# One half of a weight block loaded in a transfer of eight rows by sixteen, and VectorE's work on keys in whole tiles

## The chip, the core and the metric

The kernel runs on one core of one Trainium2 chip. The time is device microseconds (us) of one execution; the times of the kernel before are 663.4, 663.39 and 663.56 us, median 663.4. A core has five engines that each take their own instructions in order: TensorE (PE), VectorE (DVE), ScalarE (ACT), GpSimd (POOL) and SyncE (SP, which here issues almost all transfers). Sixteen DMA engines move data between the chip's large memory and the core's on-chip memory of 128 partitions.

## The reference

Decode of one token for four sequences: attention over a cache, beside a small gated MLP, both added to the input.

```python
x = A_x                                  # (4, 1, 640)
xn = _layernorm(x)
q = (xn @ wq) as 4 x 32 heads x 1 x 128  # wq (640, 4096)
scores = q . k_cache * 128 ** -0.5       # k_cache (4, 32, 4096, 128)
p = softmax(scores)
o = p . v_cache                          # v_cache (4, 32, 4096, 128)
return x + o as (4, 1, 4096) @ wo + _B_ref(xn, w_in, w_sp, b_sp, w_out)   # wo (4096, 640)
```

All inputs are bf16. K and V caches are 134 MB each, so the work is a single pass over 268 MB.

## The kernel before

**Tiles.** The 32 heads form 8 groups of 4 (HT). One tile i is one group and one sequence, hg, b = divmod(i, 4): 32 tiles. A K tile holds 4 heads x 4096 keys x 128 as 128 partitions x 128 keys x 128 (4 MB); 32 partitions (lanes) belong to each head. V tiles are laid out the same way.

**Loads.** K and V tiles share five slots (KV_SLOTS). The order is K0, K1, V0, K2, V1, K3, ... with K one tile further ahead at 24 and 28 (EXTRA_K). pump (L140) issues loads on SP as far as their slots have been used: each load waits for the last reader of the tile five loads earlier. A block of wo (512 rows, 640 KB) is loaded by load_wo (L153) for each group, into two buffers: the 128 partitions hold four rows r each, 5120 bytes in a row of memory (row p * 4 + r of the block). The last block comes in four parts.

**One tile.** Queries stand as rows (qbc), so the scores come from VectorE: product (L455) multiplies the K tile in place by the query row, fold_half (L464) adds the upper 64 of 128 columns to the lower 64, both on one half of the tile (64 keys a lane). sums (L470) lets PE add the remaining 64 columns down to 8, as eight accumulating matmuls against the identity; row_sums (L483) adds the eight on VectorE. lane_max, lay_max, spread_max and head_max (L493 to L518) find the maximum of a head over its lanes (VectorE, ACT, PE, VectorE: m, lay, max_ps, nb). exps (L520) makes p on ACT, and POOL multiplies it by a head mask into pm (L533). blocks (L542) is PE's 32 matmuls of pm with the V tile into pv_acc; after every second tile ACT copies it (pv_sb) and gather (L561) sums it up into pv.

**Groups.** After a group's last tile: group_den (the denominators, rden), group_norm (o_n), group_turn (L612), group_pick (L625) and group_proj (L643). The wo rows of a block lie over partitions as p * 4 + r, so o_n, which has the 128 columns of a head on partitions, must be laid out in the same way. group_turn does it with one matmul for each r against a 0/1 matrix spread[:, r], which takes row m * 4 + r to lane m of each head's 32 lanes; group_pick keeps on each lane the value of its own head (hmask) and sums the four heads away. group_proj multiplies by the wo block into out_ps. The last group needs no turn.

**Order.** The main loop (L677) is written out by hand, and each engine takes its instructions in that order. In iteration i: first half's product of tile i; second half's row sums, maxima and exponentials of tile i - 1, with the first half's fold of i in between; PE's sums for the first half; second product; then blocks, group_den and gather of the tile that is due; row sums of the first half and fold of the second; group_norm; PE's sums of the second half; group_turn; and pump. Which tile is due is in turns (L663): i - 1 up to i = 24, then two, later three behind. Setup runs ahead of the loop: identity, masks, the spread matrices, the layer norm, q, the MLP.

Of the kernel before, what the change touches and what calls it, by code (L numbers as in the profile page):

```python
# [9 lines left out]
FP32 = mybir.dt.float32  # L10
BF16 = mybir.dt.bfloat16
ACT = mybir.ActivationFunctionType
ALU = mybir.AluOpType
AX = mybir.AxisListType

KV_SLOTS = 5
EXTRA_K = (24, 28)
ALIGN = 512


@with_exitstack
def kernel(
# [14 lines left out]
    nc = tc.nc  # L37
    P = nc.NUM_PARTITIONS
    Bsz, Sq, D = A_x.shape
    _, H, S, Dh = A_k_cache.shape  # L40
# [8 lines left out]
    HT = 4  # L49
    HG = H // HT  # L50
    NT = HG * Bsz
    LN = P // HT
    NC = HT * S // P
    HC = NC // 2
    HD2 = Dh // 2
    RW = 8
# [13 lines left out]
    const = ctx.enter_context(tc.tile_pool(name="const", bufs=1))  # L70
    work = ctx.enter_context(tc.tile_pool(name="work", bufs=1))
    small = ctx.enter_context(tc.tile_pool(name="small", bufs=2))
    PSUM = bass.MemoryType.PSUM
    ps_s = ctx.enter_context(tc.tile_pool(name="ps_s", bufs=2, space=PSUM))
    ps_pv = ctx.enter_context(tc.tile_pool(name="ps_pv", bufs=2, space=PSUM))
    ps_m = ctx.enter_context(tc.tile_pool(name="ps_m", bufs=2, space=PSUM))
    ps_out = ctx.enter_context(tc.tile_pool(name="ps_out", bufs=1, space=PSUM))
# [12 lines left out]
    for c0, c1 in ((0, HT), (HT, DC)):  # L90
        t = slot("wq")[:, 0 : (c1 - c0) * HD].rearrange("p (c n) -> p c n", n=HD)
# [13 lines left out]
        out=w_out_sb[:, 0:NFF, :], in_=B_w_out[0 : NFF * P].rearrange("(p k) n -> p k n", k=NFF)  # L105
# [9 lines left out]
    k_tiles, v_tiles = {}, {}  # L115
# [33 lines left out]
    wo_r = A_wo.rearrange("(j p r) n -> j p (r n)", p=P, r=HT)  # L149
    wo_h = A_wo.rearrange("(j h p) n -> j p h n", p=P, h=HT)  # L150
    wo_tiles = {}

    def load_wo(j):  # L153
        wo_tiles[j] = wop.tile([P, HT, D], BF16, name="wo")
        if j == HG - 1:
            for hh in range(HT):
                nc.sync.dma_start(out=wo_tiles[j][:, hh, :], in_=wo_h[j][:, hh, :])
            return
        nc.sync.dma_start(out=wo_tiles[j][:].rearrange("p r n -> p (r n)"), in_=wo_r[j])

    pump()

# [2 lines left out]
    ident = const.tile([P, P], BF16)  # L165
    make_identity(nc, ident[:])
    ident_f = const.tile([P, P], FP32)
# [9 lines left out]
        out=lane_diag[:],  # L177
        in_=ident_f[:].rearrange("p (h l) -> p l h", h=HT),
        axis=AX.X,
        op=ALU.add,  # L180
# [12 lines left out]
    for e in range(2):  # L193
        nc.vector.tensor_reduce(
            out=sel[:, :, :, e],
            in_=ident_f[:].rearrange("p (g e k h) -> p e k h g", g=CG, e=2, k=GC)[:, e],
            axis=AX.X,
            op=ALU.add,
        )

    hmask = const.tile([P, HT], FP32)
    nc.vector.memset(hmask[:], 0.0)
    for hh in range(HT):
        nc.vector.memset(hmask[hh * LN : (hh + 1) * LN, hh : hh + 1], 1.0)
    spread = const.tile([P, HT, HT, LN], BF16)
    nc.vector.tensor_copy(
        out=spread[:],
        in_=ident[:].rearrange("p (m r) -> p r m", r=HT)[:, :, None, :].to_broadcast(
            [P, HT, HT, LN]
        ),  # L210
    )


    q_lanes = const.tile([HT * Bsz, Bsz, P], BF16)
    nc.vector.tensor_copy(
        out=q_lanes[:].rearrange("r b (h l) -> r b h l", h=HT),
        in_=ident[: HT * Bsz, : HT * Bsz]
# [7 lines left out]
    for hh in range(HT):  # L225
        nc.gpsimd.tensor_copy(
            out=place[:, hh, hh * Bsz : (hh + 1) * Bsz], in_=lane_diag[:, 0:Bsz]
# [18 lines left out]
    for i in range(NSTAT):  # L246
# [5 lines left out]
        out=rstd[:], in_=mv[:, 1:2], func=ACT.Sqrt, bias=eps_tile[:Bsz], scale=1.0  # L252
# [4 lines left out]
        out=xn_bf[:],  # L257
# [9 lines left out]
    for c in range(DC):  # L267
        nc.tensor.transpose(
            out=xnT_ps[:, c, :], in_=xn_v[:, c, :], identity=ident[:Bsz, :Bsz]
# [11 lines left out]
    for c in range(DC):  # L281
        t, i = wq_parts[c]
        for hg in range(HG):
            g = hg % CG
# [4 lines left out]
                start=(c == 0),  # L289
# [162 lines left out]
        qbcs[hg] = small.tile([P, Bsz, Dh], BF16, name="qbc")  # L452
        nc.scalar.copy(out=qbcs[hg][:], in_=qb_ps[:])

    def product(i, half):  # L455
        t = k_tiles[i][:, half * HC : (half + 1) * HC, :]
        nc.vector.tensor_tensor(  # L457
            out=t,
            in0=t,
            in1=qbcs[i // Bsz][:, i % Bsz, None, :].to_broadcast([P, HC, Dh]),  # L460
            op=ALU.mult,
        )

    def fold_half(i, half):  # L464
        t = k_tiles[i][:, half * HC : (half + 1) * HC, :]
        nc.vector.tensor_tensor(  # L466
            out=t[:, :, 0:HD2], in0=t[:, :, 0:HD2], in1=t[:, :, HD2:Dh], op=ALU.add
        )

    def sums(i, half):  # L470
        t = k_tiles[i][:, half * HC : (half + 1) * HC, :]
        s = sums_ps[i, half] = ps_s.tile([P, HC, RW], FP32, name="s_ps")
        n = HD2 // RW
        for g in range(n):
            nc.tensor.matmul(  # L475
                out=s[:],
                lhsT=ident[:],
                rhs=t[:, :, g * RW : (g + 1) * RW],
                start=(g == 0),
                stop=(g == n - 1),  # L480
            )

    def row_sums(i, half):  # L483
        if half == 0:
            scores[i] = small.tile([P, NC], FP32, name="s_sb")
        nc.vector.tensor_reduce(  # L486
            out=scores[i][:, half * HC : (half + 1) * HC],
            in_=sums_ps.pop((i, half))[:],
            axis=AX.X,
            op=ALU.add,  # L490
        )

    def lane_max(i):  # L493
# [118 lines left out]
    def group_turn(hg):  # L612

        ps = ps_m.tile([P, HT, HT, Bsz], FP32, tag="m", name="o_ps")
        for r in range(HT):
            nc.tensor.matmul(
                out=ps[:, r, :, :],
                lhsT=spread[:, r, :, :].rearrange("p h m -> p (h m)"),
                rhs=gr[hg][:].rearrange("p h b -> p (h b)"),
                start=True,  # L620
                stop=True,
            )
        gr[hg] = ps

    def group_pick(hg):  # L625
        own = small.tile([P, HT, HT, Bsz], FP32, name="own")
        nc.vector.tensor_tensor(
            out=own[:],
            in0=gr[hg][:],
            in1=hmask[:, None, :, None].to_broadcast([P, HT, HT, Bsz]),  # L630
            op=ALU.mult,
        )
        o_r = small.tile([P, HT, Bsz], BF16, name="o_r")
        with nc.allow_low_precision("one of the four is the value, the others are zeros"):
            nc.vector.tensor_reduce(
                out=o_r[:],
                in_=own[:].rearrange("p r h b -> p r b h"),
                axis=AX.X,
                op=ALU.add,
            )  # L640
        gr[hg] = o_r
# [17 lines left out]
    def at(i, fn, *args):  # L659
        if 0 <= i < NT:  # L660
            fn(i, *args)
# [10 lines left out]
    with tc.manual_schedule(engines={E.PE, E.DVE, E.Activation, E.SP}):  # L672
        stage_q(0)
        gmlp()
        used.update(occupants[:3])
        pump()
        for i in range(NT):  # L677
            j = turns.get(i)
            product(i, 0)
            at(i - 1, row_sums, 1)  # L680
            at(i - 1, lane_max)
            at(i - 1, lay_max)
            at(i - 1, spread_max)
            group(turns.get(i - 1, -1), group_pick)
            if turns.get(i - 1, -1) // Bsz < HG - 2:
                group(turns.get(i - 1, -1), group_proj)
            fold_half(i, 0)
            at(i - 1, head_max)
            at(i - 1, exps)
            sums(i, 0)  # L690
            product(i, 1)
            if i % Bsz == 2 and i // Bsz + 1 < HG:
                stage_q(i // Bsz + 1)
            due = [] if j is None else [j]
            if i == NT - 1:
                due += range(j + 1, NT - 2)
            for n, jj in enumerate(due):
                if n:
                    gather(due[n - 1])
                blocks(jj)  # L700
                group(jj, group_den)
                used.add(("v", jj))
            row_sums(i, 0)
            fold_half(i, 1)
            if due:
                gather(due[-1])
            for jj in due:
                group(jj, group_norm)
            sums(i, 1)
            for jj in due:  # L710
                group(jj, group_turn)
            used.add(("k", i))
            pump()
            if i % Bsz == 2 and i // Bsz < HG - 2:
                load_wo(i // Bsz)
        load_wo(HG - 2)
        load_wo(HG - 1)
        row_sums(NT - 1, 1)
        lane_max(NT - 1)
        lay_max(NT - 1)  # L720
        spread_max(NT - 1)
        head_max(NT - 1)
        exps(NT - 1)
        blocks(NT - 2)
        group_den(HG - 1)
        blocks(NT - 1, 0, V_CUTS[1])
        gather(NT - 1, stop=False)
        for c0, c1 in zip(V_CUTS[1:], V_CUTS[2:]):
            pairs(NT - 1, c0, c1)
        group_norm(HG - 1)  # L730
        group_proj(HG - 2)
        group_proj(HG - 1)

        res = work.tile([P, NOH], BF16, name="res")
        out_v = out.flatten_outer_dims()
        r0, r1 = slice(0, Bsz), slice(OG, OG + Bsz)
        nc.scalar.copy(out=res[r0], in_=out_ps[r0])
        nc.vector.tensor_copy(out=res[r1], in_=out_ps[r1])
        nc.scalar.dma_start(out=out_v[:, 0:NOH], in_=res[r0])
        nc.sync.dma_start(out=out_v[:, NOH:D], in_=res[r1])  # L740
# [30 lines left out]
```

## Time and profile before

| | |
|---|---|
| median of the times | 663.4 us |
| the profiled execution's own time | 663.4 us |
| its span | 661.6 us |
| VectorE busy | 491.5 us, 74% |
| TensorE busy | 348.7 us, 53%; mean granted clock 0.726 |
| GpSimd busy | 151.3 us, 23% |
| ScalarE busy | 49.3 us, 7% |
| moved by DMA | 282.57 MB, mean 427 GB/s |
| q1 (transfers issued by SP) | 11928 packets, 99.2% of 16 engines' span |

The span is from the first to the last instruction of the core; the execution's own time has a little around it. [...] In the groups by line, the number after the bar is busy us and then the mean ns of one instruction; after the second bar comes the idle time of the engine ahead of these instructions, and what ended it. In a timeline each row has start and length in us, engine, line, operation, output and input, count, and in brackets the idle time before and what released it. In the table of stretches the columns are start and end, the length, then for each of PE, PEld, DVE, ACT and POOL its busy us and number of instructions, then the granted clock, the DMA share and GB/s.

### The profile page before, as it was taken

Reading aid. Unit: us, or ns where it says so; the run is one execution under the profiler, and the core shown is the slowest. Engines: PE = TensorE matmul, PEld = TensorE weight load, DVE = VectorE, ACT = ScalarE, POOL = GpSimd, SP = SyncE. Lnnn points to the kernel's source line nnn. Section 1 sums busy time; section 2 is a strip of 40 time slices with the busy share of each in tenths; the row PEclk is TensorE's granted clock in tenths of the full one; section 3 lists DMA queues with packets and bytes.
Section 4 is the critical chain, followed back from the end, with each engine's and each line's share of the span. In section 5 each row is a group of like instructions: output and inputs, shape, how many; then the busy total and the mean of one; then the engine's idle time right before and its main releaser. Section 6 shows DMA issues by size and latency. Waiting matters only on the chain.

```text
span 661.6 us, 5115 instructions
## 1 busy us (share of the span) xinstructions
PE 348.7 (53%) x2109; PEld 144.6 (22%) x2109; DVE 491.5 (74%) x334; ACT 49.3 (7%) x138; POOL 151.3 (23%) x57
## 2 busy tenths in 40 slices
PE   2526653646445455663745654465643756435567
PEld 1402211212121121221212222121211312112124
DVE  2299797867789677788776698776787899777950
ACT  0201100001000010001000000000100000000010
POOL 3002222112222112222112222112222133122230
PEclk9999676776767777766678657777576577688585
DMA  9999999999999999999999999999999999999997
GB/s 368 432 438 429 430 440 427 440 423 434 442 416 447 424 433 442 423 440 424 433 440 423 440 428 431 442 421 442 422 435 442 422 441 428 427 442 428 429 428 289
DMA packets 11971, 282.57 MB, mean 427 GB/s; under 512 B 1344, under 2 KB 1964, under 8 KB 3244
## 3 DMA queue, kind: packets, MB, share of 16 engines
q1 hardware_dynamic: 11928, 282.25, 99.2%
q8 instruction: 16, 0.26, 0.1%
q14 instruction: 7, 0.06, 0.0%
q10 hardware_dynamic: 20, 0.01, 0.0%
HBM read 282.24 MB, written 0.01 MB: 427 GB/s over the span
## 4 chain that ended last, share of the span: by engine, by line
issue 49%; DMA 25%; POOL 15%; DVE 7%; PE 3%; SPq 1%; ACT 0%; POOLq 0%; DVEq 0%; ACTq 0%
DMA k_nat<-in_A_k_cache_dram 20%; POOL pm L533 15%; DMA wo<-in_A_wo_dram 4%; DVE k_nat L457 4%; DVE k_nat L466 2%; PE s_ps L475 2%; PE pv_acc L548 1%; SPq L123 0%; DVE s_sb L486 0%; PE out_ps L647 0%; PE pv L569 0%; POOL own_sum L593 0%; DVE m L495 0%; SPq L92 0%; SPq L104 0%
## 5 line engine op out<-in xcount | busy, mean ns | idle before, releaser
L457 DVE TENSOR_TENSOR k_nat<-k_nat,qbc 128x8192 bf16<-128x8192 bf16 x64 | 282.8, 4419 | 97.8 <-DMA k_nat<-in_A_k_cache_dram 97.8
L533 POOL TENSOR_TENSOR pm<-p,hmask_bf 128x512 bf16<-128x512 bf16 x32 | 142.5, 4452 | 490.9 <-ACT p L524 490.9
L475 PE MATMUL s_ps<-k_nat,ident 128*128 128x512 bf16 x512 | 189.2, 536 | 68.2 <-DVE k_nat L466 68.2
L466 DVE TENSOR_TENSOR k_nat<-k_nat 128x4096 bf16<-128x4096 bf16 x64 | 151.8, 2372 | 0.0
L548 PE MATMUL pv_acc<-v_nat,pm 128*32 128x512 bf16 x1008 | 88.6, 514 | 39.1 <-POOL pm L533 35.5
L508 PE MATMUL max_ps<-lay,head_scale 128*128 128x32 f32 x64 | 18.7, 383 | 171.4 <-ACT lay L501 171.4
L475 PEld LDWEIGHTS <-ident 128*128 128x128 bf16 x512 | 67.9, 135 | 171.1 <-issue 153.8
L508 PEld LDWEIGHTS max_ps<-lay,head_scale 128*128 128x128 f32 x64 | 14.6, 284 | 186.0 <-ACT lay L501 186.0
L548 PEld LDWEIGHTS <-pm 128*32 128x32 bf16 x1008 | 30.2, 120 | 96.2 <-POOL pm L533 52.0
L486 DVE TENSOR_REDUCE s_sb<-s_ps 128x64 f32<-128x512 f32 x64 | 43.3, 677 | 4.2 <-PE s_ps L475 4.2
L501 ACT ACTIVATE lay<-lane_diag,m 128x32 f32<-128x32 f32 x32 | 10.3, 321 | 395.9 <-DVE m L495 395.9
L602 DVE RECIPROCAL rden<-den 128x16 f32<-128x16 f32 x8 | 2.1, 257 | 32.2 <-PE den L600 32.2
L569 PE MATMUL pv<-sel,pv_sb 128*128 128x8 f32 x128 | 19.4, 279 | 9.3 <-ACT pv_sb L558 9.3
L569 PEld LDWEIGHTS pv<-sel,pv_sb 128*128 128x128 f32 x128 | 17.9, 217 | 17.2 <-ACT pv_sb L558 17.2
L524 ACT ACTIVATE p<-s_sb,nb 128x128 bf16<-128x128 f32 x32 | 12.9, 402 | 63.5 <-DVE nb L515 63.5
L558 ACT COPY pv_sb<-pv_acc 128x512 f32<-128x512 f32 x16 | 9.4, 585 | 91.8 <-PE pv_acc L548 91.8
L495 DVE TENSOR_REDUCE m<-s_sb 128x1 f32<-128x128 f32 x32 | 9.1, 286 | 1.1
L285 PE MATMUL q_ps<-wq,xnT 128*32 128x512 bf16 x40 | 4.5, 631 | 8.3 <-DMA wq<-in_A_wq_dram 8.3
L647 PE MATMUL out_ps<-wo,o_r 128*4 128x320 bf16 x56 | 8.0, 433 | 0.3 <-DMA wo<-in_A_wo_dram 0.3
L292 DVE CAST q_sb<-q_ps 128x512 bf16<-128x512 f32 x1 | 0.7, 691 | 9.3 <-PE q_ps L285 9.3
L515 DVE TENSOR_REDUCE nb<-max_ps 128x1 f32<-128x32 f32 x32 | 5.9, 183 | 0.9 <-PE max_ps L508 0.9
L607 DVE TENSOR_TENSOR o_n<-pv,rden 128x16 bf16<-128x16 f32 x8 | 1.3, 168 | 6.7 <-PE pv L581 6.7
(94 smaller groups left out, 91.4 us busy)
## 6 DMA issues: line engine op xcount, KB each, us to landing
k_nat<-in_A_k_cache_dram SPq DMA_DIRECT2D x32, 4096.0 KB, 37.9
v_nat<-in_A_v_cache_dram SPq DMA_DIRECT2D x31, 4096.0 KB, 33.6
wo<-in_A_wo_dram SPq DMA_DIRECT2D x7, 640.0 KB, 38.1
wq<-in_A_wq_dram SPq DMA_DIRECT2D x1, 4096.0 KB, 12.8
w_sb<-in_B_w_in_dram SPq DMA_DIRECT2D x1, 2160.0 KB, 19.5
v_nat<-in_A_v_cache_dram SPq DMA_DIRECT2D x1, 2048.0 KB, 24.5
wq<-in_A_wq_dram SPq DMA_DIRECT2D x1, 1024.0 KB, 14.8
v_nat<-in_A_v_cache_dram SPq DMA_DIRECT2D x1, 1024.0 KB
```

What stands on the lines that cost most here:

```text
L457: nc.vector.tensor_tensor(out=t, in0=t, in1=qbcs[i // Bsz][:, i % Bsz, None, :].to_broadcast([P, HC, Dh]), op=ALU.mult,)
L466: nc.vector.tensor_tensor(out=t[:, :, 0:HD2], in0=t[:, :, 0:HD2], in1=t[:, :, HD2:Dh], op=ALU.add)
L475: nc.tensor.matmul(out=s[:], lhsT=ident[:], rhs=t[:, :, g * RW : (g + 1) * RW], start=(g == 0), stop=(g == n - 1),)
L486: nc.vector.tensor_reduce(out=scores[i][:, half * HC : (half + 1) * HC], in_=sums_ps.pop((i, half))[:], axis=AX.X, op=ALU.add,)
L495: nc.vector.tensor_reduce(out=m1[:], in_=scores[i][:], axis=AX.X, op=ALU.max)
L501: nc.scalar.activation(out=d[:], in_=lane_diag[:], func=ACT.Copy, scale=maxes[i][:, 0:1])
L508: nc.tensor.matmul(out=ps[:], lhsT=head_scale[:], rhs=maxes[i][:], start=True, stop=True)
L524: nc.scalar.activation(out=p[:], in_=scores.pop(i)[:], func=ACT.Exp, bias=nb[:], scale=scale_qk, accum_out=acc[hg % NACC][:, b : b + 1],)
L533: nc.gpsimd.tensor_tensor(out=p_m[b][:, :, e : e + GC * HT].rearrange("p g (c h) -> p g c h", h=HT), in0=p[:].rearrange("p (g c) -> p g c" ...
L548: nc.tensor.matmul(out=pv_acc[g * LN : (g + 1) * LN, :], lhsT=pm[:, c // GC, :], rhs=v_nat[:, c : c + GC, :].rearrange("p c d -> p (c d)") ...
L558: nc.scalar.copy(out=pv_sb[:], in_=pv_acc[:])
L569: nc.tensor.matmul(out=pvs[hg][:, :, b - 1 : b + 1], lhsT=pv_sb[:, k * Dh : (k + 1) * Dh], rhs=sel[:, k, :, :], start=(k == 0), stop=stop ...
```

## The change

Three things are changed.

*Whole tiles.* product, fold and row_sums take all 128 keys of a lane in one VectorE instruction (128 x 16384, 128 x 8192 and 128 x 1024 elements in). PE's 16 sums of a tile follow each other, and all stand behind the blocks, group_den and gather of the due tile. They go to one PSUM tile of two banks with one buffer, in place of two buffers of one bank.

*One turned half.* Of wo block 1, rows r = 0 and 1 of each partition come in a transfer of their own whose source is read as 8 (a) x 16 (b) x 1280 elements: partition a * 16 + b gets the rows of place b * 8 + a. The other two rows of the block come in a second transfer, as before.

*Lanes to match.* For these two r of group 1, group_turn uses the matrices t_spread, and group_pick for this group a mask t_mask that for r < 2 tells a lane's head by the new order. Both are made in setup: two copies on POOL, four instructions on VectorE.

```diff
+TURNED_WO, TURNED_ROWS, TL = 1, 2, 8
...
-    ps_s = ctx.enter_context(tc.tile_pool(name="ps_s", bufs=2, space=PSUM))
+    ps_s = ctx.enter_context(tc.tile_pool(name="ps_s", bufs=1, space=PSUM))
...
-        nc.sync.dma_start(out=wo_tiles[j][:].rearrange("p r n -> p (r n)"), in_=wo_r[j])
+        rows = wo_tiles[j][:].rearrange("p r n -> p (r n)")
+        n = 0
+        if j == TURNED_WO:
+
+            n = TURNED_ROWS * D
+            nc.sync.dma_start(
+                out=rows[:, 0:n], in_=wo_r[j][:, 0:n].rearrange("(b a) n -> a b n", a=TL)
+            )
+        nc.sync.dma_start(out=rows[:, n:], in_=wo_r[j][:, n:])
...
+    TM = LN // TL
+    assert P == TL * HT * TM
+    t_spread = const.tile([P, TURNED_ROWS, P], BF16)
+    for r in range(TURNED_ROWS):
+        nc.gpsimd.tensor_copy(
+            out=t_spread[:, r, :].rearrange("p (a h m) -> p a h m", a=TL, h=HT),
+            in_=ident[:]
+            .rearrange("p (m a r) -> p r a m", m=TM, a=TL)[:, r, :, None, :]
+            .to_broadcast([P, TL, HT, TM]),
+        )
+    t_heads = const.tile([P, HT, TL], FP32)
+    nc.vector.tensor_reduce(
+        out=t_heads[:],
+        in_=ident_f[:].rearrange("p (a h m) -> p h a m", a=TL, h=HT),
...
+    t_mask = const.tile([P, HT, HT], FP32)
+    nc.vector.tensor_copy(
+        out=t_mask[:], in_=hmask[:, None, :].to_broadcast([P, HT, HT])
+    )
+    for r in range(TURNED_ROWS):
+        nc.vector.tensor_reduce(
+            out=t_mask[:, r, :], in_=t_heads[:], axis=AX.X, op=ALU.add
+        )
...
-    def product(i, half):
-        t = k_tiles[i][:, half * HC : (half + 1) * HC, :]
+    def product(i):
+        t = k_tiles[i]
...
-    def fold_half(i, half):
-        t = k_tiles[i][:, half * HC : (half + 1) * HC, :]
+    def fold(i):
+        t = k_tiles[i]
...
+    def sums(i):
+        s = sums_ps[i] = ps_s.tile([P, NC, RW], FP32, name="s_ps")
         n = HD2 // RW
...
+        for half in range(2):
+            cs = slice(half * HC, (half + 1) * HC)
+            for g in range(n):
+                nc.tensor.matmul(
+                    out=s[:, cs, :],
+                    lhsT=ident[:],
+                    rhs=k_tiles[i][:, cs, g * RW : (g + 1) * RW],
...
+    def row_sums(i):
+        scores[i] = small.tile([P, NC], FP32, name="s_sb")
         nc.vector.tensor_reduce(
...
+            out=scores[i][:], in_=sums_ps.pop(i)[:], axis=AX.X, op=ALU.add
         )
...
+            turned = hg == TURNED_WO and r < TURNED_ROWS
             nc.tensor.matmul(
                 out=ps[:, r, :, :],
-                lhsT=spread[:, r, :, :].rearrange("p h m -> p (h m)"),
+                lhsT=t_spread[:, r, :]
+                if turned
+                else spread[:, r, :, :].rearrange("p h m -> p (h m)"),
...
-            in1=hmask[:, None, :, None].to_broadcast([P, HT, HT, Bsz]),
+            in1=(t_mask[:] if hg == TURNED_WO else hmask[:, None, :].to_broadcast([P, HT, HT]))[
+                :, :, :, None
+            ].to_broadcast([P, HT, HT, Bsz]),
...
         for i in range(NT):
             j = turns.get(i)
-            product(i, 0)
-            at(i - 1, row_sums, 1)
+            product(i)
+            at(i - 1, row_sums)
             at(i - 1, lane_max)
             at(i - 1, lay_max)
             at(i - 1, spread_max)
...
-            fold_half(i, 0)
+            fold(i)
             at(i - 1, head_max)
             at(i - 1, exps)
-            sums(i, 0)
-            product(i, 1)
...
-            row_sums(i, 0)
-            fold_half(i, 1)
             if due:
                 gather(due[-1])
             for jj in due:
                 group(jj, group_norm)
-            sums(i, 1)
+            sums(i)
...
-        row_sums(NT - 1, 1)
+        row_sums(NT - 1)
```

More of the change, by code (lines that the diff above doesn't have):

```diff
@@ L211 @@
     )
+    TM = LN // TL
[12 more added lines that the diff above has]
+        in_=ident_f[:].rearrange("p (a h m) -> p h a m", a=TL, h=HT),
+        axis=AX.X,
+        op=ALU.add,
+    )
[6 more added lines that the diff above has]
+            out=t_mask[:, r, :], in_=t_heads[:], axis=AX.X, op=ALU.add
+        )
     q_lanes = const.tile([HT * Bsz, Bsz, P], BF16)
@@ L459, in product @@
             in0=t,
-            in1=qbcs[i // Bsz][:, i % Bsz, None, :].to_broadcast([P, HC, Dh]),
+            in1=qbcs[i // Bsz][:, i % Bsz, None, :].to_broadcast([P, NC, Dh]),
             op=ALU.mult,
         )
-    def fold_half(i, half):
-        t = k_tiles[i][:, half * HC : (half + 1) * HC, :]
+    def fold(i):
+        t = k_tiles[i]
         nc.vector.tensor_tensor(
@@ L468, in fold_half @@
         )
-    def sums(i, half):
-        t = k_tiles[i][:, half * HC : (half + 1) * HC, :]
-        s = sums_ps[i, half] = ps_s.tile([P, HC, RW], FP32, name="s_ps")
+    def sums(i):
+        s = sums_ps[i] = ps_s.tile([P, NC, RW], FP32, name="s_ps")
         n = HD2 // RW
[L474 to L485, printed above, removed]
+        for half in range(2):
[5 more added lines that the diff above has]
+                    rhs=k_tiles[i][:, cs, g * RW : (g + 1) * RW],
+                    start=(g == 0),
+                    stop=(g == n - 1),
+                )
+    def row_sums(i):
+        scores[i] = small.tile([P, NC], FP32, name="s_sb")
         nc.vector.tensor_reduce(
[L487 to L490, printed above, removed]
+            out=scores[i][:], in_=sums_ps.pop(i)[:], axis=AX.X, op=ALU.add
         )
```

## The prediction, made before the changed kernel was run

> **What bounds the kernel now.** The profiled execution took 663.4 us, 661.6 of them its span, as the median of the shown runs: 1.8 us lie around the span. I read the page's slices first, then the busy time by stretches of four tiles (79 us), then the timeline of one tile.
>
> ```profile
> DMA  9999999999999999999999999999999999999997
> ...
> q8 instruction: 16, 0.26, 0.1%
> q14 instruction: 7, 0.06, 0.0%
> ...
> 140.00:219.00 79.00, 40.20 (x241) 16.16 (x238) 60.38 (x36) 5.27 (x16) 18.42 (x5) 0.74 1.00 433
> ```
>
> In the last line the last two numbers are DMA share and GB/s; the third pair is VectorE, 60.4 of 79.0 us. The DMA engines have no idle time, VectorE 24%. The groups agree: VectorE's only long idle time is in front of the product, and ends with a K tile.
>
> ```profile
> L457 DVE TENSOR_TENSOR k_nat<-k_nat,qbc 128x8192 bf16<-128x8192 bf16 x64 | 282.8, 4419 | 97.8 <-DMA k_nat<-in_A_k_cache_dram 97.8
> L466 DVE TENSOR_TENSOR k_nat<-k_nat 128x4096 bf16<-128x4096 bf16 x64 | 151.8, 2372 | 0.0
> L486 DVE TENSOR_REDUCE s_sb<-s_ps 128x64 f32<-128x512 f32 x64 | 43.3, 677 | 4.2 <-PE s_ps L475 4.2
> ```
>
> So the time is that of the bytes, and only two things can change it: which DMA engine ends last, or a longer way through one tile that leaves the DMA queue empty.
>
> **The sixteen engines.** The packet records give start, length and size, but no engine. Strung together (a packet starts within 6 ns of its engine's last end; each 4 MB transfer takes every engine 9.681 us), they show 16 chains that never pause. These are the ends of the 16 parts of the last wo transfer, in ns after the first:
>
> ```
> 0 121 158 252 442 753 758 2258 | 2538 2553 2586 2658 2791 2807 2828 2832
> ```
>
> The landings of the last wo blocks (656.60 to 658.27 us) release the 16 closing matmuls; behind them come only the copy and the output. The eight late chains are, as far as I can tell the chains apart, those that carry q8's 16 instruction packets of 16 KB (two each, 1.42 us a time). The 2258 is one chain hit by three 8 KB packets of q14, at 33.4, 295.5 and 549.1 us, for 0.96, 0.84 and 0.84 us; VectorE had then executed 51, 188 and 323 of 384 instructions, so I take it for VectorE's own fetching.
>
> **The turned half.** A transfer whose outermost count is 4 (x_bf) shows four data packets and four completion packets, so the new one, with 8, should use eight engines. The chain of 158 carries x_bf and also the two 2-byte loads; 252 and 2258 follow x_bf packets too; the fourth I can't tell. None of the three is one of the late eight, so I take the turned eight to be the other eight. wo block 1 costs an engine 8 x 193 ns + 6 = 1550 now (5120 B; 1280 B take 52; for 2560 B I take 99, on the line between them; half of 193 and twice 52 bound it, 96 to 104). Afterwards the eight have 16 + 8 packets, 24 x 99 + 12 = 2388, which is +0.84 us; the others 8 x 99 + 6 = 798, which is -0.75 us. The late eight end at 2832 - 753 = 2079, and the largest of the early, 758, at 1596.
> [...]
>
> **VectorE's instructions.** Each tile loses a product, a fold and a row sum; setup gains four. Its program falls from 386 instructions to 294, so the fetch at its 323rd is gone: the 2258 chain ends at 2258 - 835 + 838 = 2261, the last of all. 2261 - 2832 = **-0.57 us** (-0.45 to -0.63 by the bounds of the packet).
>
> **Whole tiles.** Product and fold cost 150 ns beside 2 elements a cycle, the row sum 1.04 ns an element (4419 for 8192, 2281 for 4096, 677 for 512), so whole ones take 8.68, 4.41 and 1.21 us (at least 8.53, 4.27 and 1.07 without any fixed part, at most two halves, 8.84, 4.56 and 1.35; I take the line through three shapes). What VectorE saves stands beside its idle time: nothing. But the order gets longer. Row sums of tile i stand behind the whole product of i+1, and PE's 16 sums of i behind the blocks of i-1, which wait for pm; behind waiting row sums VectorE holds max, fold and nb, and for nb wait p, pm and the next blocks. One tile of before:
>
> ```profile
> 339.18 4.43 DVE L457 TENSOR_TENSOR k_nat<-k_nat,qbc 128x8192 bf16<-128x8192 bf16 x1 [4.36 <-DMA k_nat<-in_A_k_cache_dram]
> ...
> 346.64 0.18 DVE L515 TENSOR_REDUCE nb<-max_ps 128x1 f32<-128x32 f32 x1
> 346.74 4.41 DVE L457 TENSOR_TENSOR k_nat<-k_nat,qbc 128x8192 bf16<-128x8192 bf16 x1
> ...
> 347.49 4.56 POOL L533 TENSOR_TENSOR pm<-p,hmask_bf 128x512 bf16<-128x512 bf16 x1 [14.82 <-ACT p L524]
> ...
> 352.10 1.91 PE L548 MATMUL pv_acc<-v_nat,pm 128*32 128x512 bf16 x32 [1.82 <-POOL pm L533]
> ```
>
> pm begins 0.75 us after a product and ends 0.9 us after that product's end, in 31 of 32 tiles. In the one without a product beside it, it is four times as fast:
>
> ```profile
> 643.88 1.04 POOL L533 TENSOR_TENSOR pm<-p,hmask_bf 128x512 bf16<-128x512 bf16 x1 [9.10 <-ACT p L524]
> ```
>
> So pm stands still while VectorE multiplies. Afterwards, from a K landing: product 8.60 (start to next start), row sums 1.24, max 0.21, fold 4.33 = 14.4; nb to pm 0.85: pm is ready at 15.2 us. The next K lands at 19.4, so VectorE is idle and pm takes 1.04 (one row only; at 4.56 rival 2 would begin). Blocks 3.6 at the slow clock, on odd tiles pv_sb and gather 1.75, then 16 sums at 4.0 to 7.1 (two halves at 1.97 or 3.55): done by 24 to 29 us; the next row sums are due at 28. A us too late is covered by the 4 us between pm and the K. At a group's end o_n keeps the next product back by some 3 us; its pm is still 2 to 3 us ahead of the K after it. K's slot comes free 3 to 8 us later than now; issue to landing is 37.9 us against 9.7 of transfer, so some 28 us (24 for V) of queue cover it. If that cover goes, every us is paid.
> From tile 24 the blocks lag by two tiles or more, and the loop is open.
>
> The narrowest place is the first tile, as K0 and K1 land one after the other:
>
> ```profile
> 34.46 4.42 DVE L457 TENSOR_TENSOR k_nat<-k_nat,qbc 128x8192 bf16<-128x8192 bf16 x1 [3.44 <-DMA k_nat<-in_A_k_cache_dram]
> 38.92 2.29 DVE L466 TENSOR_TENSOR k_nat<-k_nat 128x4096 bf16<-128x4096 bf16 x1
> ...
> 55.72 0.18 DVE L515 TENSOR_REDUCE nb<-max_ps 128x1 f32<-128x32 f32 x1
> ...
> 63.44 4.43 DVE L457 TENSOR_TENSOR k_nat<-k_nat,qbc 128x8192 bf16<-128x8192 bf16 x1 [0.16 <-DMA k_nat<-in_A_k_cache_dram]
> ```
>
> 34.46 + 8.72 + 4.33 (tile 0) + 8.60 + 1.24 + 0.21 + 4.33 = 61.9 for nb, pm at 62.74. K2's product starts at 63.44: pm is ahead by 0.7 us.
>
> **The rest costs nothing:** two small POOL copies in the idle time before place (5.46 us), four VectorE instructions before xnT (8.27 us), all long before K0; two masked or spread operands of the same sizes; one more DMA issue on SP, 0.4 us (estimate from its neighbours) with 24 us of queue below it. One PSUM buffer in place of two: sums of i wait for row sums of i-1, which end over 4 us earlier.
>
> **Sum:** 663.4 - 0.57 = **662.8 us**. The closing PE work (2.3 us from the first of the last wo landings) may meet the other clock: 0.5 us either way.
>
> **Rivals.**
> 1. *The turned rows fall on late engines.* The 2553 to 2832 chains gain 0.84: 663.4 + 0.56 to 0.84, about 664.1. For: one x_bf engine and the four beyond x_bf's are unknown. Against: three known ones are all early.
> 2. *pm comes too late, slower.* If pm of tile 0 is not begun when K2's product starts, it waits that product out: ready to end 9.5 us in place of 1.04. Then sums, row sums and nb are late, K3 is there already, its product starts at once, and pm waits again: the state feeds itself. From nb to nb: 0.1 + 8.6 + 0.9, blocks 3.6, sums 5.4, 1.24 + 0.21 + 4.33 = 24.4; odd 26.1; a group's end, where pm is free, 22.3. Four tiles take 97 us, not 79.0. Over 23 tiles (5.75 fours) that is 104, less some 12 us of queue: about 755 us. It decides at 0.7 us in 28 of worked-out VectorE time. For: at the price of two halves the chain is 0.8 us longer, and the lead is gone. Against: the line fits three shapes within 0.02 us, and K2 always lands three transfers, 29.04 us, behind K0.
> 3. *No eight engines:* if the transfer uses all 16, only the fetch goes, and the late eight stay: 663.4.
> 4. *VectorE's third fetch stays*, if it is not tied to the instruction's number: that chain ends at 2258 + 838 = 3096, 0.26 us later than now: 663.7. Against: the three fetches are 137 and 135 instructions apart.
> [...]
>
> **Chances.** Forecast 0.64 (662.3 to 663.3); rival 1 0.13; rival 2 0.12; rivals 3 and 4 0.03 each; more than 0.2% gained at the end by the full clock 0.05. A difference of 0.2% (1.3 us) is what this kernel's measurement can tell from none. The forecast and rivals 1, 3 and 4 are within it, 0.83; 0.02 of that I give to the edges: faster 0.06, same 0.81, slower 0.13. The range takes these four in, 662.1 to 664.4; rival 2 is left out.
>
> **What would show it.** The last wo landings spread over 2.3 us, not 2.8; the turned transfer has eight completion packets; two fetches in VectorE's chain; pm mostly 1.04 us, DMA share 1.00 in every stretch. Wrong if pm is 9.5 us and DMA has gaps (rival 2), or the spread is over 3.3 us (rival 1).

## The result, and the profile after

The changed kernel takes **666.12 us** (median of 10 runs) against 663.55 us before (median of 10): ratio 1.0045, 95% interval 1.003 to 1.0059. That is slower by 2.6 us, where 662.8 had been predicted (range 662.1 to 664.4). The profiled execution took 666.14 us, 664.3 of them its span. Ratios and intervals, here and below, leave out executions in a slow state and are not the quotients of the medians.

What the prediction said of VectorE and GpSimd came out. In the groups by line of the changed kernel (busy us, mean ns of one, idle time ahead of it):

```profile
L493 DVE TENSOR_TENSOR k_nat<-k_nat,qbc 128x16384 bf16<-128x16384 bf16 x32 | 278.2, 8695 | 87.8 <-DMA k_nat<-in_A_k_cache_dram 87.8
L502 DVE TENSOR_TENSOR k_nat<-k_nat 128x8192 bf16<-128x8192 bf16 x32 | 141.3, 4415 | 0.0
L566 POOL TENSOR_TENSOR pm<-p,hmask_bf 128x512 bf16<-128x512 bf16 x32 | 56.6, 1769 | 583.5 <-ACT p L557 568.3
L522 DVE TENSOR_REDUCE s_sb<-s_ps 128x128 f32<-128x1024 f32 x32 | 39.0, 1218 | 10.4 <-PE s_ps L512 10.4
```

8.68, 4.41 and 1.21 us had been forecast, 8.70, 4.42 and 1.22 came. pm now takes 1.04 us in 29 of 32 tiles. The narrowest place, the first tile (start, length, engine), is passed as worked out, pm first and K2's product 0.73 us behind it (forecast 0.7):

```profile
62.50 1.04 POOL L566 TENSOR_TENSOR pm<-p,hmask_bf 128x512 bf16<-128x512 bf16 x1 [54.45 <-ACT p L557]
```
```profile
61.70 0.18 DVE L548 TENSOR_REDUCE nb<-max_ps 128x1 f32<-128x32 f32 x1
63.23 8.86 DVE L493 TENSOR_TENSOR k_nat<-k_nat,qbc 128x16384 bf16<-128x16384 bf16 x1 [1.34 <-DMA k_nat<-in_A_k_cache_dram]
```

The time is lost elsewhere. The slices and queues of the page:

```profile
DMA  9999999999999999999999999999999999999996
GB/s 371 426 442 429 425 438 439 422 439 436 424 424 404 430 429 438 424 439 434 432 428 438 425 438 433 429 433 430 434 435 432 430 435 428 433 438 431 431 425 261
...
q8 instruction: 16, 0.26, 0.1%
q14 instruction: 6, 0.05, 0.0%
```

The DMA engines are as busy as before in every slice but the last (6 tenths, not 7), and one packet of q14, which the prediction took for VectorE's third fetch, is gone (6, not 7). But the 13th slice (199 to 216 us) moves 404 GB/s. In the stretch that the prediction showed of before (share 1.00, 433 GB/s), the last two numbers are now:

```profile
140.00:219.00 79.00, 37.32 (x238) 16.16 (x238) 58.91 (x24) 5.16 (x16) 4.57 (x6) 0.69 1.00 424
```

So the DMA engines are busy and move less: 9 GB/s over 79 us are 0.71 MB, at 433 GB/s 1.6 us. The *busy share* does not show the loss, 1.00 in both rows; the bytes beside it do. Narrowed to rows of three microseconds, where the turned transfer runs, with one row of the kernel before behind them:

```profile
196.00:199.00 3.00, 1.45 (x16) 0.61 (x20) 0.00 (x0) 0.39 (x2) 1.21 (x2) 0.50 1.08 413
199.00:202.00 3.00, 2.58 (x29) 1.06 (x17) 0.26 (x1) 0.58 (x1) 0.00 (x0) 0.73 0.87 201
202.00:205.00 3.00, 3.00 (x18) 1.70 (x19) 2.19 (x2) 0.00 (x0) 0.00 (x0) 1.00 1.21 500
```
```profile
199.00:202.00 3.00, 2.58 (x8) 0.97 (x8) 1.99 (x3) 0.00 (x0) 0.00 (x0) 0.65 1.06 450
```

(Such a row counts a packet where it begins, so single rows swing; 201 against 450 GB/s in the same row of before does not come from that.) The packet records say what happens there. The first 41 packets of 2,560 B take 102 ns each, from 198.29 to 198.93 us. From then until 202.0 us 170 of 180 take 146 to 255 ns (median 188), and the 32,768-byte packets of the K and V tiles, which take 1,213 ns in nearly all of the run ("K packets" below), up to 2,382. Some 190 packets of 2,560 B are slow, and the turned transfer has only 128: the plain half beside it is slow too, and so are the tiles. Everything under way is slow at once, on the turned transfer or not: of the packets that begin between 199.0 and 201.9 us, all 168 of 2,560 B take 138 ns or more, and all five of 32,768 B 1,441 ns or more. The lengthening, added up over all packets of that time and divided by 16, is 1.60 us an engine.

At the end, the landings of the last wo part (us after the first of them) stand so:

```
before   0 0.09 0.10 0.18 0.41 0.69 0.74 2.23 2.46 2.51 2.53 2.57 2.72 2.73 2.76 2.81   last at 658.27
after    0 0.96 1.39 1.67 1.68 1.97 2.45 2.50 2.55 2.61 2.84 2.86 3.10 3.14 3.93 4.50   last at 660.80
```

The spread is 4.5 us, not the 2.3 forecast, and over the 3.3 that was to speak for rival 1. The closing matmuls wait for the last landings of the wo blocks and start 2.60 us later than before (first row before, second after):

```profile
656.64 1.23 PE L647 MATMUL out_ps<-wo,o_r 128*4 128x320 bf16 x8 [0.28 <-DMA wo<-in_A_wo_dram]
659.24 1.23 PE L685 MATMUL out_ps<-wo,o_r 128*4 128x320 bf16 x8 [0.92 <-DMA wo<-in_A_wo_dram]
```

### The profile page after: what moved, and what is told of

Same layout as the page of the kernel before. It is cut to its first block, busy times and chain, and to the rows that moved or that the text cites. A ratio compares the mean times of both kernels' runs of the same rounds, so it can differ in the third digit from the quotient of the medians.

```text
span 664.3 us, 5049 instructions
## 1 busy us (share of the span) xinstructions
PE 321.9 (48%) x2109; PEld 144.7 (22%) x2109; DVE 483.1 (73%) x242; ACT 48.4 (7%) x138; POOL 63.8 (10%) x59
## 2 busy tenths in 40 slices
DMA packets 12106, 282.57 MB, mean 425 GB/s; under 512 B 1352, under 2 KB 1972, under 8 KB 3380
## 4 chain that ended last, share of the span: by engine, by line
issue 62%; DMA 18%; DVE 8%; PE 7%; POOL 4%; ACT 1%; SPq 0%; POOLq 0%; ACTq 0%; DVEq 0%
DMA k_nat<-in_A_k_cache_dram 12%; DMA wo<-in_A_wo_dram 4%; POOL pm L566 4%; PE s_ps L512 3%; DVE k_nat L493 3%; DVE k_nat L502 3%; DMA wq<-in_A_wq_dram 2%; PE pv_acc L581 2%; DVE s_sb L522 1%; PE pv L602 1%; PE q_ps L321 1%; PE out_ps L685 0%; ACT p L557 0%; DVE m L528 0%; ACT pv_sb L591 0%
## 5 line engine op out<-in xcount | busy, mean ns | idle before, releaser
L493 DVE TENSOR_TENSOR k_nat<-k_nat,qbc 128x16384 bf16<-128x16384 bf16 x32 | 278.2, 8695 | 87.8 <-DMA k_nat<-in_A_k_cache_dram 87.8
L581 PE MATMUL pv_acc<-v_nat,pm 128*32 128x512 bf16 x1008 | 107.7, 603 | 92.6 <-POOL pm L566 91.2
L512 PE MATMUL s_ps<-k_nat,ident 128*128 128x512 bf16 x512 | 140.9, 438 | 20.6 <-DVE k_nat L502 20.6
L502 DVE TENSOR_TENSOR k_nat<-k_nat 128x8192 bf16<-128x8192 bf16 x32 | 141.3, 4415 | 0.0
L566 POOL TENSOR_TENSOR pm<-p,hmask_bf 128x512 bf16<-128x512 bf16 x32 | 56.6, 1769 | 583.5 <-ACT p L557 568.3
L512 PEld LDWEIGHTS <-ident 128*128 128x128 bf16 x512 | 55.5, 113 | 104.8 <-issue 57.2
L581 PEld LDWEIGHTS <-pm 128*32 128x32 bf16 x1008 | 34.3, 135 | 147.3 <-POOL pm L566 97.5
L522 DVE TENSOR_REDUCE s_sb<-s_ps 128x128 f32<-128x1024 f32 x32 | 39.0, 1218 | 10.4 <-PE s_ps L512 10.4
L485 PE MATMUL qbc_ps<-q_rows,q_lanes 16*128 16x128 bf16 x32 | 4.6, 296 | 25.9 <-ACT q_rows L482 25.9
L485 PEld LDWEIGHTS <-q_lanes 16*128 16x128 bf16 x32 | 3.3, 121 | 27.4 <-DVE nb L548 22.5
```

The source lines that it names most:

```text
L493: nc.vector.tensor_tensor(out=t, in0=t, in1=qbcs[i // Bsz][:, i % Bsz, None, :].to_broadcast([P, NC, Dh]), op=ALU.mult,)
L502: nc.vector.tensor_tensor(out=t[:, :, 0:HD2], in0=t[:, :, 0:HD2], in1=t[:, :, HD2:Dh], op=ALU.add)
L512: nc.tensor.matmul(out=s[:, cs, :], lhsT=ident[:], rhs=k_tiles[i][:, cs, g * RW : (g + 1) * RW], start=(g == 0), stop=(g == n - 1),)
L522: nc.vector.tensor_reduce(out=scores[i][:], in_=sums_ps.pop(i)[:], axis=AX.X, op=ALU.add)
L566: nc.gpsimd.tensor_tensor(out=p_m[b][:, :, e : e + GC * HT].rearrange("p g (c h) -> p g c h", h=HT), in0=p[:].rearrange("p (g c) -> p g c" ...
L581: nc.tensor.matmul(out=pv_acc[g * LN : (g + 1) * LN, :], lhsT=pm[:, c // GC, :], rhs=v_nat[:, c : c + GC, :].rearrange("p c d -> p (c d)") ...
```

## The experiments

**Theories.** *Destination*: it supposes that engines that write into one group of partitions hold each other up, that in plain transfers each engine has a group of its own, and that the turned transfer, with 16 partitions in a row for an engine, sends it into the groups of others. *Source*: rows 40,960 B apart read slowly. *Small packets*: eight engines with many 2,560-byte packets, or engines that fall back to where the late ones are, are slow by themselves. *Whole tiles*: VectorE's longer instructions cost it. And rival 1 of the prediction, late engines among the eight, with or without one of these. The packet records name neither an engine nor a partition: which partitions an engine writes, here, below and in the expectations, is my estimate from the order of the transfer's rows, no run shows what forms a group, and the runs can only bear the theory out.

All medians below come beside runs of the kernel before on the same chip: 663.6 us (medians 663.60 to 663.64).

### Which part of the change

```diff
# whole_only: the changed kernel with
-TURNED_WO, TURNED_ROWS, TL = 1, 2, 8
+TURNED_WO, TURNED_ROWS, TL = -1, 2, 8
# turn_only: the kernel before, with the turned transfer, t_spread and t_mask
```

> Only the whole tiles; wo block 1 comes in one plain transfer (the lanes' matrices are still made, nothing uses them). If the turned transfer costs the 2.6 us: about 663.4 us, no 1,213 ns packet of a K tile over 1,700 ns, and the landings of the last wo part 2.8 us apart as before, since nothing favours the late eight engines. If VectorE's longer instructions cost it (a rival): about 666 us, and a DMA share under 1.00 in some stretch.

Measured: **663.57 us**, ratio 0.9993 (0.9981 to 1.0005). No slow packets; the last landings are 3.0 us apart, the last at 658.37. The whole tiles cost nothing and bring nothing.

> Half tiles as before, with the turned half and its lanes. If the turned transfer costs the 2.6 us: 666.1 us, and up to 666.4 because VectorE's third fetch stays; the slow packets (2,560 B in some 190 ns, 32,768 B in some 2,000) around 200 us again. If the whole tiles cost it: 662.8 to 663.4 us.

Measured: **666.16 us**, 1.0044 (1.0028 to 1.0061). Slow packets again, 1.47 us an engine in packets that begin between 199.0 and 204.0 us. The turned half is the whole loss, and the theory of whole tiles is out.

### Source or destination

```diff
# eight_ports: four transfers, lanes permuted to match
+            for x in range(HT):
+                ps = slice(x * LN, (x + 1) * LN)
+                nc.sync.dma_start(
+                    out=rows[ps, 0:n],
+                    in_=wo_r[j][ps, 0:n].rearrange("(c a) n -> a c n", a=TL),
+                )
# eight_near: near rows
-                out=rows[:, 0:n], in_=wo_r[j][:, 0:n].rearrange("(b a) n -> a b n", a=TL)
+                in_=bass.AP(tensor=..., offset=..., ap=[[15 * HT * D, TL], [HT * D, P // TL], [1, n]]),
```

> The changed kernel, but the transfer's source is 8 x 16 rows that follow each other (engine a reads rows 15a to 15a+15; so the rows in these lanes are not the right ones), while the destination stays 16 partitions for each engine. Destination theory: slow packets as in the changed kernel, about 666 us. Source theory: 102 ns packets and 662.8 us. Small packets on eight engines slow by themselves: 666 us.

Measured: **666.27 us**, 1.0054 (1.0034 to 1.0075; six executions), slow packets from 198.96 us, 1.54 us an engine. The order of the rows in memory made no difference (1.60 in the changed kernel); the source theory is out.

> The same eight engines, the same 2,560-byte packets, the same source rows 40,960 B apart for each engine, but in four transfers of 32 partitions, so that engine a writes partitions 4a to 4a+3 of each 32 in place of 16a to 16a+15; lanes permuted to match, nothing left out. Destination theory (engines that write into the same group of partitions hold each other up): 2,560-byte packets at 102 ns, K packets at 1,213 ns throughout, landings of the last wo part 2.3 us apart, 662.8 us. [...] Source theory (rows 40,960 B apart read slowly) and the theory that small packets on eight engines are slow by themselves: about 666 us and 190 ns packets, as in the changed kernel.

Measured: **665.75 us**, 1.0034 (1.0022 to 1.0047). That misses what I had expected: 1.36 us an engine of slow packets. But they came later. The packets ran at 102 ns from 198.45 to 199.88 us, twice as long as in the changed kernel, and turned slow when the eight engines, by the number of packets done, were coming to the last two of the four transfers, those into partitions 64 to 127. I had laid the eight out so that each keeps to four partitions of every 32, and taken it that so they would not meet one another, which was an estimate; and I had forgotten the other eight, whose K packets run beside them. The next pair takes that apart.

### The pair that decides

Whole tiles, plain wo block 1, and ahead of it the same small transfers as extra bytes into a tile that nothing reads, once in partitions 0 to 63, once in 64 to 127.

```diff
+    spare = const.tile([P, HT * D], BF16)
...
+        if j == 1:
+            for half in range(2):
+                cs = slice(half * 2 * D, (half + 1) * 2 * D)
+                for x in range(0, 2):        # spare_high: range(2, 4)
+                    ps = slice(x * LN, (x + 1) * LN)
+                    nc.sync.dma_start(
+                        out=spare[ps, cs],
+                        in_=wo_r[j][ps, cs].rearrange("(c a) n -> a c n", a=TL),
+                    )
```

> Whole tiles and the plain wo block 1, and ahead of it the four small transfers of the run with four transfers (same eight engines, 128 packets of 2,560 B, source rows 40,960 B apart), now extra bytes into a tile that nothing reads, all in partitions 0 to 63. Destination theory: these eight engines serve partitions 0 to 63 in a plain transfer anyway, so nobody else is hit: 102 ns packets, K packets at 1,213 ns; the eight early engines end 1.6 us later (16 x 99 + 4 x 9), which brings them to 2.4 us of the late eight's 2.8: about 663.6 us (up to 663.9, if an engine hit by VectorE's fetches is among them). If eight engines with small packets are slow by themselves, or because they fall back to where the late eight are: slow window around 200 us, about 666 us, the same as its twin.

> Its twin: the same four transfers with the same engines, packets and source stride, but into partitions 64 to 127, which a plain transfer leaves to the other eight engines. Destination theory: collisions with the late eight's own K tile, 2,560-byte packets at about 190 ns after some 0.6 us, K packets over 1,800 ns, about 666 us. The other theories: the same as its twin.

Measured: spare_low **665.37 us**, 1.0025 (1.0007 to 1.0043); spare_high **667.93 us**, 1.0059 (1.004 to 1.0077). Both times lie nearly 2 us above what I had expected, but the packets tell the two apart. The same three microseconds of the two, spare_low first:

```profile
199.00:202.00 3.00, 2.79 (x23) 1.11 (x15) 0.26 (x1) 0.58 (x1) 0.00 (x0) 0.50 1.09 450
202.00:205.00 3.00, 3.00 (x12) 2.15 (x13) 1.22 (x2) 0.00 (x0) 0.00 (x0) 0.50 0.99 423
```
```profile
199.00:202.00 3.00, 3.00 (x26) 1.14 (x18) 0.00 (x0) 0.43 (x1) 0.00 (x0) 0.50 1.13 256
202.00:205.00 3.00, 2.79 (x11) 2.13 (x12) 1.14 (x3) 0.15 (x1) 0.00 (x0) 0.50 0.98 252
```

In spare_low all 128 small packets take 102 ns. In spare_high 104 of 128 are slow (median of these 202 ns), so are 108 of the 128 of 5,120 B behind them (370 ns in place of 196), and K packets reach 2,267; together 2.8 us an engine. Packets, bytes and source steps are the same in both; the partitions differ, and with them the source rows (0 to 63, 64 to 127 of the block). The theory of small packets and of engines falling back is out: spare_low has both. spare_pairs below reads the same rows as spare_low in the same order for each engine, and closes the gap that the rows leave.

spare_low says a second thing. It is 1.8 us slower than whole_only without a slow packet, where 0 to 0.3 had been expected. Its last landings are

```
whole_only   0 0.06 0.10 0.28 0.44 0.76 1.10 1.71 2.64 2.66 2.74 2.78 2.90 2.92 2.96 3.01   last at 658.37
spare_low    0 0.72 1.52 1.59 1.97 2.01 2.48 2.50 2.59 2.65 2.75 2.76 2.86 3.20 4.21 4.31   last at 659.69
```

Two landings lie 1.6 us beyond the group of late ones, the price of 16 packets (16 x 99 + 36 ns = 1.62): two of the eight engines are late ones. An early engine with that work would have ended at 1.71 + 1.62 = 3.33 at most. And 0 and 0.72 are early engines that did not take part, which leaves six early ones and two late.

### Plain halves, and sixteen engines

```diff
# split_plain: lanes as before
-                out=rows[:, 0:n], in_=wo_r[j][:, 0:n].rearrange("(b a) n -> a b n", a=TL)
+                out=rows[:, 0:n], in_=wo_r[j][:, 0:n]
# sixteen_turned
-TURNED_WO, TURNED_ROWS, TL = 1, 2, 8
+TURNED_WO, TURNED_ROWS, TL = 1, 2, 16
```

> Both halves of wo block 1 in plain transfers of 16 engines, 2,560 B a packet; lanes as in the kernel before, nothing left out. Destination theory: no slow packets, 663.6 us. If half rows of 2,560 B out of 5,120 are slow by themselves: slow packets, 665 to 666 us.

Measured: **663.84 us**, 1.0009 (0.9987 to 1.0031); all 256 packets of 2,560 B take 102 ns. Half rows are not slow.

> The turned half as 16 rows by eight (source rows 81,920 B apart), so that all 16 engines take part with eight packets each and no engine gets more than the others; lanes permuted to match. If engine a then writes partitions 8a to 8a+7, destination theory: two engines at a time in a group of partitions, so slow packets and some 665 us. If the slow packets came of eight engines falling back behind the others: none here, 663.6 us. If an engine writes the same partitions as in a plain transfer: also 663.6 us, and the run tells nothing.

Measured: **665.06 us**, 1.0022 (1.0002 to 1.0041), 191 of 256 small packets slow, 1.37 us an engine. That two engines meet at a time is the theory's reckoning; no run shows how many do. If all 16 engines take eight of the turned packets each, as the expectation has it, none has more work than another, and this is the clash alone. (The profiled execution itself took 669.28 us; the last section says why.)

### Sizes

```diff
# low_swap: spare_low with
+    nc.gpsimd.memset(wo_tiles[1][:, 0:2, :], 0.0)
-        n = 0
+        n = 2 * D if j == 1 else 0
# four_rows
-TURNED_WO, TURNED_ROWS, TL = 1, 2, 8
+TURNED_WO, TURNED_ROWS, TL = 1, 4, 8
# spare_pairs: spare_low with, for each half,
+                    out=spare[0:64, cs],
+                    in_=wo_r[j][0:64, cs].rearrange("(c a) n -> a c n", a=TL),
```

> The turned half's work on the engines without its clash: rows 0 and 1 of wo block 1 are not loaded (their lanes hold zeros, set once in setup, so the output lacks them); the same number of bytes goes by the same eight engines into partitions 0 to 63 of a tile that nothing reads, rows 2 and 3 come plain. Bytes as in the kernel before; each of the eight has 24 packets of 2,560 B and five completions, 0.87 us more than now, each of the others 0.75 us less. My reading now: two of these eight are among the late ones, so the last landing comes 0.87 us later than with whole tiles alone, 664.4 us, without slow packets; what is left up to 666.1 is then the clash of destinations. If all eight are early, as I had predicted: 662.8 to 663.0 us. If there is no separate clash: 666 us.

Measured: **664.69 us**, 1.0022 (1.0011 to 1.0034), all small packets at 102 ns, last landing at 659.28, 0.91 us behind whole_only. So the turned half without its clash costs 1.1 us; the changed kernel's other 1.4 are the clash. (Of the 1.1, 0.2 lie behind the last landing: to its end the profiled execution took another 5.39 us, that of whole_only 5.16.)

> All four rows of wo block 1 turned, 16 packets of 5,120 B on eight engines, none on the others, lanes permuted to match; nothing left out. If the clash is paid by the byte: slow window about twice as long as in the changed kernel (3.1 us), and 663.6 + 1.6 (packets on two late engines) + 3.4 (clash, twice 1.7) = some 668.5 us. If it is a stumble of fixed length: 663.6 + 1.6 + 1.7 = 666.9 us.

Measured: **668.48 us**, 1.0079 (1.0067 to 1.0091; five executions), slow packets 3.6 us an engine. Twice the bytes and 2.25 times the clash (3.6 against 1.60): in these two kernels it goes about by the byte, and is no stumble of fixed length.

```profile
199.00:202.00 3.00, 2.73 (x30) 0.95 (x18) 0.24 (x1) 0.49 (x1) 0.00 (x0) 0.65 1.02 252
202.00:205.00 3.00, 2.85 (x17) 1.79 (x18) 1.77 (x3) 0.10 (x1) 0.00 (x0) 1.00 1.07 256
```

> The extra bytes again into partitions 0 to 63 by eight engines, but in two transfers of 64 partitions, so that engine a writes partitions 8a to 8a+7. [...] If a group is eight neighbours, each engine is alone in its own: 102 ns packets, 665.4 us as with four transfers of 32 partitions.

Measured: **667.28 us**, 1.0076 (1.0046 to 1.0106; six executions), 94 of 128 small packets slow. The row in which they begin moves 266 GB/s:

```profile
205.00:208.00 3.00, 2.58 (x27) 1.02 (x20) 0.26 (x1) 0.58 (x1) 0.00 (x0) 0.70 1.00 266
```

Engine a reads rows a, a + 8, ... a + 56 here, in the same order as in spare_low, and the 64 partitions written are the same too. Only the share of them that each engine writes differs (and two completions in place of four). That bears the destination theory out. The partitions 0 to 63 alone are no cure: it matters which ones an engine gets. By the order of the rows, all 128 packets took 102 ns where each of the eight engines keeps to 4a to 4a+3 of every 32 (spare_low), and 94 of 128 were slow where it gets 8a to 8a+7 (spare_pairs). Eight neighbours are not the group, then: 102 ns and 665.4 us had been expected for that. What the group is, these runs do not show.

### The sum

Each time is whole_only's 663.57, plus the added work of the two late engines among the eight (packets of 99 and 193 ns as in the prediction, a completion at 6 to 9 ns), plus the lengthening an engine read from that kernel's packet records:

```
                 late engines   lengthening   sum      measured
changed kernel   0.84           1.60          666.0    666.12
turn_only        0.84           1.47          665.9    666.16
eight_near       0.84           1.54          666.0    666.27
eight_ports      0.87           1.36          665.8    665.75
low_swap         0.87           0             664.4    664.69
spare_low        1.62           0             665.2    665.37
spare_high       1.62           2.80          668.0    667.93
spare_pairs      1.60           1.86          667.0    667.28
split_plain      0.05           0             663.6    663.84
sixteen_turned   0.05           1.37          665.0    665.06
four_rows        1.55           3.60          668.7    668.48
```

All eleven are within some 0.3 us, most of them a little short of the measured time. The clash stands in this sum as measured; nothing here forecasts its size but the bytes (four_rows). None beats the kernel before by more than the measurement can tell.

### A look back at the kernel before

```diff
-    nc.sync.dma_start(out=w_out_sb[:FT, NFF, :], in_=B_w_out[NFF * P : Fh])
+    nc.gpsimd.memset(w_out_sb[:FT, NFF, :], 0.0)
```

> A look at the kernel before: its setup loads the last 96 rows of w_out in a transfer of 96 partitions, six to an engine; here those rows are zeros from a memset instead (so the output lacks them), 0.12 MB less. If such an odd split clashes too: the 15 K packets of 1,386 ns at 22.3 to 23.3 us are gone (0.17 us a DMA engine), and with the bytes (0.28 us) the time is 663.1 us. If those packets are only the beginning of the K stream: they stay, 663.3 us.

Measured: **663.07 us** against 663.62, 0.9986 (0.9973 to 0.9999). The 15 long packets are gone: between 22 and 26 us every K packet takes 1,213 ns. They came of this transfer, then. That it is the same clash, because 96 partitions do not fall on the sixteen engines as 128 do, is my estimate: no run loaded the same bytes in another split. A quarter us or so of the 0.55 is the bytes that are not loaded (0.12 MB at the 433 GB/s of before: 0.28 us).

## Why the prediction was wrong, point by point

Between 662.8 and 666.12 us lie 3.3: 1.4 are the clash, 1.1 the turned half's work on two late engines, and the rest the gain of 0.57 that was not made and a base of 663.57 in place of 663.4.

- **What bounds the kernel: right.** The last landing sets the time, and what happens at 200 us is still there at 660: the last wo part lands 2.53 us later, the closing matmuls start 2.60 later, and the time is 2.6 longer.
- **Eight engines: right.** Rival 3 falls: the changed kernel has 8 packets of 4 bytes more (1,352 under 512 B, not 1,344), as the prediction's eight would have. That each stands for an engine is its reading of x_bf's four and four.
- **"So I take the turned eight to be the other eight": wrong.** Three known engines stood for eight, and no run shows that x_bf's are among the eight at all. Two of the eight are late ones, so rival 1 came true, with its price: 0.84 forecast, 0.91 in low_swap's last landing, 1.1 in its time. Its chance, 0.13, was too small for five engines that the text itself called unknown.
- **The step that failed most: the packets' price, 24 x 99 ns, taken from packets that meet nobody.** For such packets it was right (102 ns as recorded, which overlap by some 3). It was bounded from both sides by sizes (96 to 104 ns) and never by what the transfer meets where it writes. The clash was not in the sum at all, at nothing, and no rival had it: 1.4 us by times (666.12 - 664.69), 1.6 an engine in the packets. The trace of before does not show it at 200 us, but the 15 packets of some 1,386 ns behind the 96-partition transfer at 22.3 us were there to be seen. Of the splits into all 128 partitions that were run, only the plain one kept its packets: split_plain's halves take 102 ns in all 256, and sixteen_turned, with as many packets of that size, had 191 slow.
- **-0.75 us for the late engines:** overtaken. In the changed kernel all that was under way between 199.0 and 201.9 us was slow; packets of a tile that take 1,213 ns elsewhere took up to 2,382.
- **VectorE's third fetch: right.** It is gone: one packet of q14 less, and the two that I take for VectorE's now come after 63 and 191 of its instructions. It brings nothing by itself, as whole_only shows (663.57 us) and as the sum had it. Rival 4 falls.
- **Whole tiles: right in what was read above,** three durations within 0.02 us (the "2 elements a cycle" under them is 0.52 ns an element, from 2,281 ns for 4,096 and 4,419 for 8,192; no trace shows VectorE's cycle), pm at 1.04, the first tile's margin at 0.73. Rival 2 did not come.
- **"DMA share 1.00 in every stretch" as a sign of health: too weak.** It held, with 9 GB/s missing.

## What to carry to other kernels

When a transfer's shape is changed, read how long its packets take, and those of the other transfers beside it: here the same bytes into the same 64 partitions took 102 ns a packet in one split (spare_low) and were slow in 94 of 128 in another (spare_pairs), and in the changed kernel tile packets went from 1,213 to as much as 2,382 ns. Read GB/s beside the DMA share, because the share stayed at 1.00 here while 424 GB/s were moved in place of 433. And where a gain hangs on which engines get the work, a few known ones are no basis for the rest.

## What the runs showed that was not expected

- **A small transfer slowed all that the core loaded beside it.** In spare_high 328 KB go into partitions 64 to 127 in small packets; the core moves some 254 GB/s for 6 us, where spare_low moves 450 and 423. It begins some 0.6 us after the first of the small packets (198.29 to 198.93 us in the changed kernel). What is held back where, no run here shows.
- **In some executions the engines stay in a slower step.** In the profiled executions of sixteen_turned and spare_pairs, K packets took 1,359 and 1,396 ns from 23 us, directly behind the 96-partition transfer, to some 64 and 71 us (in that of turn_only to 32 us). That the 96-partition transfer starts it is likely by its place, and not shown. These two stretches cost 4.6 and 6.4 us an engine and are why those executions took 669.28 and 673.49 us of their own, far above their medians. For sixteen_turned, and the kernel before:

```profile
23.00:63.00 40.00, 11.26 (x98) 6.23 (x96) 30.78 (x27) 3.60 (x6) 0.00 (x0) 0.59 0.99 382
```
```profile
23.00:63.00 40.00, 18.51 (x139) 8.29 (x138) 31.86 (x33) 4.09 (x8) 4.55 (x1) 1.00 1.00 432
```

Single executions 4 to 6 us above the rest occur in the kernel before too (668.14 and 669.31 us). Without that transfer (no_tail) the times of 11 executions lie between 662.94 and 663.25 us. That does not show that the step cannot come there: whole_only, which has the transfer, also has 11 executions without one so long. What ends the stretch stays open.
